# First layer of a recurrent-attention-plus-feed-forward kernel: the contraction of 384 split into seven products with 128-row and 64-row tiles

## The chip, the cores and the metric

The kernel runs on one core of one Trainium2 chip. The metric is the device time of one execution in microseconds (us). Everything is computed in float32. TensorE multiplies a stationary tile (`lhsT`, at most 128 rows by 128 columns) with a moving tile (`rhs`) and accumulates in PSUM; VectorE (DVE), ScalarE (ACT) and GpSimd (POOL) do the element work; SP and ACT issue the DMAs.

## The reference

Two blocks follow one another. The first is a recurrence over 768 tokens for 4 batches and 8 heads of size 48:

```
for t in range(S):
    cur = einsum('bhd,bhe->bhde', u * kt, vt)
    y[:, :, t] = einsum('bhd,bhde->bhe', rt, state + cur)
    state = wt[..., None] * state + einsum('bhd,bhe->bhde', kt, vt)
```

Its output, seen as `x` of 3072 tokens by 384, goes through a feed-forward block: `h = x @ w_in` (384 to 2048), `g = h * sigmoid(h)`, `out = g @ w_out` (2048 to 384).

## The kernel before

The work is cut into 12 units. A unit is 128 tokens of two batches, so 256 rows of `x`. A unit has an attention stage (the recurrence in a logarithmic form over levels 0 to 6, with masks), a first layer (`ups`) and a second layer (`downs`). The order of all instructions is written by hand: the loop over `i` from 3 to 11 takes the attention stage of unit `i` as a list of groups (`mix(i)`), and between the groups it puts steps of the second layer of unit `i - 2` and then the first layer of unit `i - 1`; `room` says how many steps follow each group. Every engine runs its own instructions in that order. After the loop come the second layer of unit 10, and the first and second layers of unit 11, with no attention beside them.

The second layer is a matrix product in seven quarter-size products instead of eight (`quarter`, numbered here q0 to q6; line 1156), for units 1 to 11. It needs sums of activations (`sums`, L1127) on DVE. The results of the products share PSUM banks: q0, q2, q4 and q6 accumulate into one bank, and between them ACT or DVE copies the partial sum out (L1161, L1164). So q4 can start only when ACT's copy after q2 is done.

The first layer of units 0 to 2 is plain (`up`, L1011). From unit 3 on (`NFAST = 3`) it is `first_layer` (L1065): `w_in` and `x` have three chunks of 128 rows. Chunks 0 and 1 form the two halves of a seven-product scheme over (half of the 2048 columns) x (chunk) x (batch). The third chunk is multiplied plainly, as four more products, named by where they are accumulated: in `p7`, `p3`, `p4` and `n1`. Every matmul there takes 128 rows, 64 columns of weights and 128 tokens; two neighbours fill the lower and the upper 64 columns of the array. A "block" below is 8 such matmuls of one half of the features; the trace shows each float32 matmul as two records, so a block is 16 records. There are 11 products of two blocks each, 22 blocks a unit.

`keep_banks` gives the first layer four PSUM banks (`h0`, `h1`, `o0`, `o1`). Partial results are copied by ACT (L1074), added by DVE (L1077) and put through Silu by ACT (L1080, L1082). The sums of `x` that the scheme needs are `sums_of_x` (L1039, DVE); those of the weights are `in_weight_sums` (L1032, DVE, once).

The attention stage meets TensorE at `burst(i, 3)` and `burst(i, 5)` (L692: 48-row by 64-column tiles, 64 moving columns, a row tile for each head parity), at `turn_apart` (L811), `y_state` (L835, L842), `y_values` (L856) and `update` (L896). Between burst 3 and burst 5 the keys of the next levels go from ACT (`odd_keys`, L604) to POOL (`grow_keys`, L634) and the queries through DVE (L616, L771) and ACT (L773). After burst 5, ACT copies scores out of PSUM (`keep_level`, L792), and `y_state` waits for that. `move_x` brings the attention's output into the layout of `x` by ten DMAs, from ACT's queue (L928), two in group 0 and eight in group 1. `load_blocks` (L127), `load_values` (L140, L147), `load_rk` (L157) and the outputs (L1170) are on SP's queue. `block_bonus` (L491, POOL) and `block_sum` (L525, DVE) make the terms inside blocks of eight tokens.

Of the kernel before, what the change touches and what calls it, by code (L numbers as in the profile page):

```python
# [38 lines left out]
def kernel(  # L39
# [56 lines left out]
    WRK = {"w": 0, "r": 1, "k": 2}  # L96
    vt, vq, whole = {}, {}, {}
# [32 lines left out]
    def load_values(i):  # L130
        n, b0 = units[i]
        t0 = n * L

        rooms = [pin.tile([128, H * D + PD - D], F32, name=name, bufs=2) for name in ("vt", "vq")]
        if n == 0:
            for room in rooms:
                nc.vector.memset(room[:, H * D:], 0.0)
        whole[i] = rooms
        vt[i], vq[i] = (room[:, 0:H * D].rearrange("p (h d) -> p h d", h=H) for room in rooms)
        nc.sync.dma_start(out=vt[i], in_=v[b0, :, t0:t0 + L, :].rearrange("h t d -> t h d"))  # L140
        if i < NTOK:
            nc.sync.dma_start(out=vq[i], in_=v[b0 + 1, :, t0:t0 + L, :].rearrange("h t d -> t h d"))
            return

        for g in range(4):
            t1 = t0 + L - (g + 1) * 32
            nc.sync.dma_start(out=vq[i][g * 32:(g + 1) * 32], in_=v[b0 + 1, :, t1:t1 + 32, :].rearrange("h t d -> t h d"))  # L147
# [666 lines left out]
    def turn_k(i):  # L814
        both_kq = pt.tile([128, NB, NP, 2 * PD], F32, name="kq", bufs=1)
        for b in range(NB):
            kq[i, b] = both_kq[:, b]
        for e, have in enumerate(apart[i]):
            nc.scalar.copy(out=both_kq[:, :, :, PD * e:PD * e + D], in_=have)
# [46 lines left out]
    def x_products(i, b):  # L866

        if b == 0:
            xt[i] = pt.tile([128, KC, TU], F32, name="xt", bufs=1)
# [18 lines left out]
    def update(i, b):  # L888
# [5 lines left out]
        for p in range(NP):  # L894
            for e in range(2):
                nc.tensor.matmul(p_kv[i][PD * e:PD * e + D, b, p, :], lhsT=kq[i, b][:, p, PD * e:PD * e + D],  # L896
# [17 lines left out]
    def move_x(i, first=0, last=None, queue=nc.sync):  # L914

        if i not in xt:
            xt[i] = pt.tile([128, KC, TU], F32, name="xt", bufs=1)
        moves = []
        for h in range(H):
            at = h * D  # L920
            while at < (h + 1) * D:
                end = min((h + 1) * D, (at // 128 + 1) * 128)
                row = PD * (h % 2) + at - h * D
                moves.append((xt[i][at % 128:at % 128 + end - at, at // 128, :],
                              yt[i][row:row + end - at, h // 2].rearrange("p b t -> p (b t)")))
                at = end
        for to, have in moves[first:last]:
            queue.dma_start(out=to, in_=have)  # L928

# [8 lines left out]
    def mix(i):  # L938
# [15 lines left out]
        def start(j):  # L954
# [4 lines left out]
                (sums, i - 1, FH // 2 - 2 if i - 1 < NFAST else 0), *both(update, i), *at(not ahead, (move_x, i))]]  # L959
# [24 lines left out]
        if i + 1 < len(units):  # L984
            loads.insert(len(loads) // 2, (load_values, i + 1))
# [36 lines left out]
    HALF = DF // 2  # L1022
    whole_w = raw[:, 1].rearrange("p x b h d -> p x (b h d)")
    in_sums = [whole_w[:, WRK["r"]], const.tile([128, HALF], F32, name="in_sum"), whole_w[:, WRK["w"]]]
    a11, a12, a13 = (w_in_sb[:, c, 0:HALF] for c in range(KC))
    a21, a22, a23 = (w_in_sb[:, c, HALF:DF] for c in range(KC))
    x_sums = [spare[:, at + x * L:at + (x + 1) * L] for x in range(3)] + [const.tile([128, L], F32, name="x_sum")]

    def in_weight_sums(which):
        out, one, two, op = ((in_sums[0], a21, a22, ALU.add), (in_sums[1], in_sums[0], a11, ALU.subtract),  # L1030
                             (in_sums[2], a12, in_sums[1], ALU.subtract), (a21, a11, a21, ALU.subtract))[which]
        nc.vector.tensor_tensor(out=out, in0=one, in1=two, op=op)  # L1032

    def sums_of_x(i):

        (b11, b12), (b21, b22), (b31, b32) = (tuple(xt[i][:, c, b * L:(b + 1) * L] for b in range(NB)) for c in range(KC))
        d1, d2, d4, d3 = x_sums
        for out, one, two in ((d1, b12, b11), (d2, b22, d1), (b12, b22, b12), (d4, b21, d2), (d3, b31, b32)):
# [10 lines left out]
    def first_layer(i, half, *names):  # L1049

        (b11, b12), (b21, b22), (b31, b32) = (tuple(xt[i][:, c, b * L:(b + 1) * L] for b in range(NB)) for c in range(KC))
        d1, d2, d4, d3 = x_sums
        s1, s2, s4 = in_sums
        for name in names:
            place, first, last, pairs = {
                "p1": ("x", True, True, [(a11, b11)]), "p6": ("x", False, True, [(s2, d2)]), "p7": ("x", False, True, [(a21, b12), (a23, b32)]),
                "p4": ("x", False, True, [(a22, d4), (a23, d3)]), "p5": ("y", True, True, [(s1, d1)]),
                "p3": ("y", False, True, [(s4, b22), (a13, b32)]), "p2": ("z", True, False, [(a12, b21)]),
                "n1": ("z", False, True, [(a13, b31)])}[name]
            p = kept[{"x": ("h0", "h1"), "y": ("o0", "h0"), "z": ("o1", "o1")}[place][half]][:].rearrange("p (q t) -> p q t", q=4)  # L1060
            for n, (left, right) in enumerate(pairs):
                for q in range(4):
                    for h in (0, PD):
                        f = (4 * half + q) * 128 + h
                        nc.tensor.matmul(p[h:h + PD, q, :], lhsT=left[:, f:f + PD], rhs=right, start=first and n == 0 and q == 0,  # L1065
                                         stop=last and n == len(pairs) - 1 and q == 3, skip_group_check=True)

            def g(x, b):
                if (i, x, b, half) not in gt:
                    gt[i, x, b, half] = pt.tile([128, 4, L], F32, name="gt", bufs=FC // 2)  # L1070
                return gt[i, x, b, half]

            if name in ("p1", "p6", "p5"):
                nc.scalar.copy(out=g(*{"p1": (0, 0), "p6": (0, 1), "p5": (1, 1)}[name]), in_=p)  # L1074
            elif name in ("n1", "p7", "p3"):
                to = g(*{"n1": (0, 0), "p3": (0, 1), "p7": (1, 1)}[name])
                nc.vector.tensor_tensor(out=to, in0=p, in1=to, op=ALU.add)  # L1077
                if name == "p3":
                    gt[i, 0, 1, half] = p
                nc.scalar.activation(out=gt[i, 0, 1, half] if name == "p3" else to, in_=to, func=AF.Silu)  # L1080
            elif name == "p4":
                nc.scalar.activation(out=g(1, 0), in_=p, func=AF.Silu)  # L1082

    def out_room(b):
# [3 lines left out]
        return temps.rearrange("p a b e -> p (a b e)").bitcast(F32)[:, 4 * FH * L:4 * FH * L + DM]  # L1088
# [18 lines left out]
    quarters = temps.rearrange("p a b e -> p (a b e)").bitcast(F32)[:, 0:4 * FH * L].rearrange("p (s f t) -> p s f t", s=4, f=FH)  # L1107
# [7 lines left out]
    def sums(i, m):  # L1115

        if i >= NFAST:
            lower, upper = ([gt[i, x, b, m] for b in range(NB)] for x in range(2))
            lower, upper = ([t[:, :, :] for t in have] for have in (lower, upper))
            s1, s2, s3, s4 = (quarters[:, x, 4 * m:4 * m + 4, :] for x in range(4))  # L1120
        else:
            lower, upper = (gt[i, x].rearrange("p a (b t) -> p b a t", b=NB) for x in (m, m + FH // 2))
            lower, upper = ([have[:, b] for b in range(NB)] for have in (lower, upper))
            s1, s2, s3, s4 = (quarters[:, x, 2 * m:2 * m + 2, :] for x in range(4))
# [191 lines left out]
```

## Time and profile before

| what | value |
|---|---|
| times of three executions | 588.58, 589.61, 592.87 us |
| median | 589.61 us |
| profiled execution, span from first to last instruction | 588.6 us (the profile lists no other time for it) |
| granted TensorE clock | 1.000 |
| busy TensorE matmul / weight load | 573.7 / 533.3 us |
| busy VectorE / GpSimd / ScalarE | 455.7 / 354.1 / 264.2 us |
| L1156, three groups of the page, busy | 88.8 + 59.9 us, and the smaller ones |
| L1065, two groups of the page, busy | 62.8 + 46.9 us, and the smaller ones |
| L1011, busy | 66.1 us |

The page gives busy times by engine and by line; a line's busy time on TensorE is the time during which at least one of its matmuls ran. Because matmuls overlap, the cost of a block is read best from the timeline, as the distance from its start to the start of the next block. "PEld" is the weight load; a wait shown there is a wait of TensorE's queue for an operand or a bank.

### The profile page before, as it was taken

How to read it: one execution, taken by the hardware profiler on the slowest of the kernel's cores; microseconds unless marked ns; L12 is line 12 of the kernel's file. 1: busy time of each engine (PE TensorE's matmuls, PEld its weight loads, DVE VectorE, ACT ScalarE, POOL GpSimd, SP SyncE). 2: the span in 40 equal slices, each digit the busy share in tenths (PEclk: the TensorE clock that was granted, in tenths of full speed). 3: DMA queues.
4: the chain of work that ended last, by engine and by line, in shares of the span. 5: the costliest groups of instructions: out<-in, count | busy, mean ns of one | idle time of the engine just before them, and what ended most of it. 6: DMA issues, size and time to landing. Idle time of an engine off the chain costs nothing.

```text
span 588.6 us, 19384 instructions
## 1 busy us (share of the span) xinstructions
PE 573.7 (97%) x8070; PEld 533.3 (91%) x8070; DVE 455.7 (77%) x703; ACT 264.2 (45%) x582; POOL 354.1 (60%) x415
## 2 busy tenths in 40 slices
PE   8989999999999999999999999999999989999997
PEld 8767876798899989999999989999999989999997
DVE  7979789998898898787788898888678797861150
ACT  5679694431531561561561561460470462370320
POOL 5989778357768478287486496485676677500000
PEclk9999999999999999999999999999999999999999
DMA  9957785343432643544543544444354460100000
GB/s 231 311 122 195 167 244 82 47 86 70 102 68 39 133 71 53 131 66 75 114 68 60 123 62 68 105 75 73 85 100 71 95 102 27 38 7 24 28 3 26
DMA packets 203383, 53.70 MB, mean 91 GB/s; under 512 B 186784, under 2 KB 195104, under 8 KB 203296
## 3 DMA queue, kind: packets, MB, share of 16 engines
q1 hardware_dynamic: 197360, 48.73, 41.0%
q10 hardware_dynamic: 5936, 3.74, 2.4%
q8 instruction: 63, 1.03, 0.8%
q14 instruction: 24, 0.20, 0.1%
HBM read 43.21 MB, written 5.24 MB: 82 GB/s over the span
## 4 chain that ended last, share of the span: by engine, by line
PE 76%; SPq 5%; DVE 5%; POOL 4%; DMA 4%; ACT 3%; issue 1%; ACTq 1%; POOLq 0%; DVEq 0%
PE p_o L1156 26%; PE p_h L1065 16%; PE p_o L1065 8%; PE p_h L1011 8%; PE p_h L1156 4%; PE p_m L1095 4%; PE p_m L856 2%; PE p_sc L692 2%; DVE score L561 2%; SPq L127 2%; PE p_m L835 2%; DMA vq<-in_v_dram 2%; ACT score L792 2%; POOL w_in_sb L259 2%; POOL tk L634 1%
## 5 line engine op out<-in xcount | busy, mean ns | idle before, releaser
L634 POOL TENSOR_TENSOR tk<-tk,tw 128x256 f32<-128x256 f32 x128 | 91.3, 734 | 42.8 <-ACT tk L604 27.6
L491 POOL TENSOR_TENSOR ruk<-tokens_rk 128x768 f32<-128x768 f32 (+1 forms) x32 | 53.6, 1687 | 70.9 <-DVE block_sums L525 36.6
L1156 PE MATMUL p_o<-own,temps 128*128 128x192 f32 x528 | 88.8, 327 | 1.3 <-ACT partial L1161 1.3
L1156 PEld LDWEIGHTS p_o<-own,temps 128*128 128x128 f32 x528 | 86.0, 190 | 2.5 <-ACT partial L1161 2.4
L1011 PE MATMUL p_h<-xt,w_in_sb 128*128 128x256 f32 x288 | 66.1, 384 | 1.7 <-POOL w_in_sb L259 1.5
L1065 PE MATMUL p_h<-xt,w_in_sb 128*64 128x128 f32 x1008 | 62.8, 274 | 0.4 <-issue 0.4
L1011 PEld LDWEIGHTS p_h<-xt,w_in_sb 128*128 128x128 f32 x288 | 53.6, 190 | 10.0 <-POOL w_in_sb L259 2.4
L1156 PE MATMUL p_o<-w_out_sb,gt 128*128 128x192 f32 x340 | 59.9, 329 | 0.2 <-DVE temps L1127 0.2
L616 DVE TENSOR_TENSOR tr<-tr,tw 128x512 f32<-128x512 f32 x61 | 57.3, 939 | 2.6 <-PE p_m L692 2.1
L1065 PEld LDWEIGHTS p_h<-xt,w_in_sb 128*64 128x64 f32 x1008 | 55.8, 137 | 2.0 <-issue 0.9
L1156 PEld LDWEIGHTS p_o<-w_out_sb,gt 128*128 128x128 f32 x340 | 55.3, 190 | 2.0 <-issue 1.2
L1161 ACT COPY partial<-p_o 128x192 f32<-128x192 f32 x33 | 10.6, 320 | 95.7 <-PE p_o L1156 46.5
L406 POOL TENSOR_TENSOR tw<-tw 128x256 f32<-128x256 f32 (+6 forms) x83 | 40.0, 482 | 17.7 <-DVE tw L360 13.8
L1065 PE MATMUL p_o<-xt,w_in_sb 128*64 128x128 f32 x720 | 46.9, 273 | 0.0
L604 ACT COPY tk<-tk 128x256 f32<-128x256 f32 x52 | 21.2, 407 | 53.8 <-POOL tk L634 49.2
L1065 PEld LDWEIGHTS p_o<-xt,w_in_sb 128*64 128x64 f32 x720 | 40.8, 137 | 0.0
L1074 ACT COPY gt<-p_h 128x512 f32<-128x512 f32 x45 | 26.2, 582 | 30.4 <-PE p_h L1065 30.4
L1080 ACT ACTIVATE gt<-gt 128x512 f32<-128x512 f32 x36 | 22.7, 631 | 34.1 <-DVE gt L1077 33.9
L710 DVE COPY_PREDICATED score<-mask,p_sc 128x512 f32<-128x512 int8 x42 | 31.3, 800 | 5.8 <-PE p_sc L692 5.5
L1077 DVE TENSOR_TENSOR gt<-p_o,gt 128x512 f32<-128x512 f32 x27 | 18.4, 683 | 19.4 <-PE p_o L1065 19.4
L1077 DVE TENSOR_TENSOR gt<-p_h,gt 128x512 f32<-128x512 f32 x27 | 18.6, 687 | 17.3 <-PE p_h L1065 16.2
L643 POOL TENSOR_TENSOR tk<-tk,tw 128x256 f32<-128x256 f32 x32 | 30.9, 986 | 0.0
(225 smaller groups left out, 1272.0 us busy)
## 6 DMA issues: line engine op xcount, KB each, us to landing
w_out_sb<-in_moe_w_in_dram SPq DMA_DIRECT2D x6, 768.0 KB, 7.1
w_out_sb<-in_moe_w_out_dram SPq DMA_DIRECT2D x4, 768.0 KB, 5.1
own<-in_moe_w_out_dram SPq DMA_DIRECT2D x4, 768.0 KB, 5.8
tokens_rk<-in_r_dram SPq DMA_DIRECT2D x8, 384.0 KB, 4.4
tokens_rk<-in_k_dram SPq DMA_DIRECT2D x8, 384.0 KB, 5.3
tokens_w<-in_w_dram SPq DMA_DIRECT2D x8, 384.0 KB, 6.4
raw<-in_w_dram SPq DMA_DIRECT2D x80, 32.0 KB, 2.3
raw<-in_k_dram SPq DMA_DIRECT2D x80, 32.0 KB, 2.1
```

Of the source, the lines that this page charges most:

```text
L406: engine.tensor_tensor(out=up, in0=t[:, :, 0::2], in1=t[:, :, 1::2], op=ALU.mult)
L491: mul = lambda out, one, two: nc.gpsimd.tensor_tensor(out=out, in0=one, in1=two, op=ALU.mult)
L616: nc.vector.tensor_tensor(out=odd, in0=odd, in1=tw[i][l][:, :, 0::2][:, :, :, None].to_broadcast([128, Q, L >> (l + 1), c]), op=ALU.mult)
L634: nc.gpsimd.tensor_tensor(out=out, in0=have, in1=odd_products(i, l, b, *blocks), op=ALU.mult)
L643: nc.gpsimd.tensor_tensor(out=have, in0=have, in1=odd_products(i, l, b, [2, NP * ni]), op=ALU.mult)
L710: nc.vector.copy_predicated(out=dst, mask=masks[l][:, :, None].to_broadcast([128, NB, NP, ni, c]), data=sc[e].rearrange("p (b q) (i c) -> ...
L1011: nc.tensor.matmul(p_h[:, a, :], lhsT=w_in_sb[:, c, f * 128:(f + 1) * 128], rhs=xt[i][:, c, :], start=(c == 0), stop=(c == KC - 1))
L1065: nc.tensor.matmul(p[h:h + PD, q, :], lhsT=left[:, f:f + PD], rhs=right, start=first and n == 0 and q == 0, stop=last and n == len(pairs) ...
L1074: nc.scalar.copy(out=g(*{"p1": (0, 0), "p6": (0, 1), "p5": (1, 1)}[name]), in_=p)
L1077: nc.vector.tensor_tensor(out=to, in0=p, in1=to, op=ALU.add)
L1095: nc.tensor.matmul(po[i, b], lhsT=gt[i, f // 2][:, f % 2, b * L:(b + 1) * L], rhs=w_out_sb[:, f, :], start=(f == 0), stop=(f == FC - 1))
L1156: nc.tensor.matmul(p, lhsT=left(f), rhs=right[:, f, :], start=which in (0, 1, 3) and f == 0, stop=f == FH - 1, skip_group_check=True)
```

## The change

The third chunk of 128 rows is split in two halves of 64 rows, and one half is put with chunk 0, the other with chunk 1. So the seven-product scheme covers all 384 rows (192 + 192), and the four plain products are gone. Each of the seven products has 16 matmuls with 128 rows as before ("whole rows") and 16 matmuls with 64 rows ("half rows"). For those, the features' first half takes rows 0 to 63 and its second half takes rows 64 to 127, and they alternate with the lower and upper 64 columns, so that four neighbours lie in four different quarters of the array; the two row halves write different PSUM banks. In `p2`, `p5` and `p3` half rows come first, in the others whole rows.

What this needs beside it: `x` gets a fourth room, in which chunk 2's halves lie in both row halves (`spread_x`, two ACT copies); `move_x` has eleven DMAs; blocks of `w_in`'s third chunk change places between the row halves once (`swap_out` on SP, `swap_in` on ACT); `sums_of_x` has four operations on 256 columns instead of five on 128 and moves from group 3 to group 4; of the four weight sums, now 1024 + 512 columns each, two go to POOL. Rooms are found by keeping three instead of four quarters of `sums` (the fourth goes over the result of `p3`), and one room for the values instead of two. From unit 5 on block loads are spread over the groups by a table; `load_values(i)` is issued in the stage that uses it. The first layer is seven steps, so `room` changes.

```diff
+    x_rooms = const.tile([128, KC + 1, TU], F32, name="x_rooms")
+    s1_room = const.tile([128, HALF + BW], F32, name="in_sum")
+    value_rooms = const.tile([128, NB, H * D], F32, name="values")
...
-        rooms = [pin.tile([128, H * D + PD - D], F32, name=name, bufs=2) for name in ("vt", "vq")]
+        have = s1_room if i == 1 else value_rooms.rearrange("p x d -> p (x d)")
+        rooms = [have[:, b * H * D:(b + 1) * H * D] for b in range(NB)]
...
+        ends = [128, 256, 384] if i < NFAST else [128, 256, 320, 384]
...
+    def spread_x(i):
+        lower, upper = slice(0, PD), slice(PD, 2 * PD)
+        nc.scalar.copy(out=x_rooms[upper, 2], in_=x_rooms[lower, 2])
+        nc.scalar.copy(out=x_rooms[lower, 3], in_=x_rooms[upper, 3])
...
+        if i > NPAIR:
+            for place, some in enumerate(("w", "ww", "wvr", "r", "", "rr", "k", "k", "k", "k")):
...
-        for out, one, two in ((d1, b12, b11), (d2, b22, d1), (b12, b22, b12), (d4, b21, d2), (d3, b31, b32)):
+        for out, one, two in ((d1, b12, b11), (d2, b22, d1), (b12, b22, b12), (d4, b21, d2)):
...
-    def first_layer(i, half, *names):
-                "p1": ("x", True, True, [(a11, b11)]), "p6": ("x", False, True, [(s2, d2)]), "p7": ("x", False, True, [(a21, b12), (a23, b32)]),
-                "p4": ("x", False, True, [(a22, d4), (a23, d3)]), "p5": ("y", True, True, [(s1, d1)]),
-                "p3": ("y", False, True, [(s4, b22), (a13, b32)]), "p2": ("z", True, False, [(a12, b21)]),
-                "n1": ("z", False, True, [(a13, b31)])}[name]
+    def first_layer(i, name):
+            "p1": ("h", True, a11, b11, False), "p2": ("o", True, a12, b21, True), "p6": ("h", False, s2, d2, False),
+            "p5": ("o", True, s1, d1, True), "p7": ("h", False, a21, b12, False), "p3": ("o", False, s4, b22, True),
+            "p4": ("h", False, a22, d4, False)}[name]
+        whole_rows = [(half, q, h, slice(0, 128), left[0][:, half * BW + q * 128 + h:half * BW + q * 128 + h + PD], right[:, 0])
+                      for half in range(2) for q in range(4) for h in (0, PD)]
+        half_rows = [(half, q, h, rows, left[1][rows, q * 128 + h:q * 128 + h + PD], right[rows, 1])
+                     for q in range(4) for h in (0, PD) for half, rows in enumerate((slice(0, PD), slice(PD, 128)))]
+        for n, part in enumerate((half_rows, whole_rows) if turned else (whole_rows, half_rows)):
...
-            order = (((0, "p1"), (0, "p5"), (0, "p2")), ((0, "p6"), (0, "n1"), (1, "p1")), ((0, "p7"), (0, "p3")),
-                     ((0, "p4"), (1, "p2"), (1, "p6")), ((1, "p5"), (1, "n1")), ((1, "p7"),), ((1, "p3"),), ((1, "p4"),))
+            made = [[(first_layer, i, name)] for name in ("p1", "p2", "p6", "p5", "p7", "p3", "p4")]
...
-            groups[3].append((sums_of_x, i - 1))
+            groups[3].append((spread_x, i - 1))
+            groups[4].append((sums_of_x, i - 1))
...
+        if i == NFAST + 1:
+            groups[0].append((swap_in, 0))
+            groups[2].insert(0, (in_weight_sums, 3))
+            groups[3].insert(0, (in_weight_sums, 1))
+            groups[5].append((in_weight_sums, 2))
-        room = (1, 1, 0, 2, 1, 1, 1, 1, 1, 2, 2, 1, 1) if i < NPAIR else (2, 1, 2, 2, 1, 1, 1, 2, 1, 1, 1)
+        room = (1, 1, 0, 2, 1, 1, 1, 1, 1, 2, 2, 1, 1) if i < NPAIR else (2, 1, 2, 2, 1, 1, 1, 1, 1, 1, 1)
```

## The prediction

> **What bounds the kernel now.** I read the page first. Its engine line and the first row of its slices say that TensorE is busy from end to end at full clock; its chain that ended last is three quarters TensorE.
>
> ```profile
> PE 573.7 (97%) x8070; PEld 533.3 (91%) x8070; DVE 455.7 (77%) x703; ACT 264.2 (45%) x582; POOL 354.1 (60%) x415
> ...
> PE   8989999999999999999999999999999989999997
> ```
>
> So the change is worth what it does to TensorE's own time plus what it adds or takes away in waits. For the first I went to the timeline of TensorE around a burst of unit 7 (start, duration, then the group with its count of records):
>
> ```profile
> 337.32 1.04 PE L1065 MATMUL p_h<-spare,raw 128*64 128x128 f32 x16
> 338.19 1.04 PE L1065 MATMUL p_o<-xt,w_in_sb 128*64 128x128 f32 x16
> 339.16 0.69 PE L692 MATMUL p_sc<-tr,tk 48*64 48x64 f32 x32
> 339.68 0.65 PE L692 MATMUL p_m<-tr,tk 48*64 48x64 f32 x32
> 340.25 1.97 PE L1065 MATMUL p_h<-xt,w_in_sb 128*64 128x128 f32 x32
> 342.05 1.04 PE L1065 MATMUL p_h<-xt,raw 128*64 128x128 f32 x16
> ```
>
> Starts are what counts, since durations overlap. A block of 16 records costs 338.19 - 337.32 = 0.87 us. Going over to the 48-row tiles makes the block before it 339.16 - 338.19 = 0.97. The 32 records of L692 have 64 moving columns instead of 128; the first 32 take 0.52, the next 0.57, and the two L1065 blocks behind them 1.80 instead of 1.74.
>
> The second view is the waits, longest first. TensorE's, after the first units, are few:
>
> ```profile
> PEld p_m L835 <- ACT score L792: 3.8, 7, 1.4
> ...
> PEld p_o L1156 <- ACT partial L1161: 2.4, 4, 1.1
> ```
>
> The rest of a unit's 45 us is the second layer (seven products of 2.6 us, 18.2), the first layer (22 x 0.872 = 19.2) and some 7 us of attention. The kernel is at TensorE's floor for this list of matmuls; DVE and POOL have idle time, but their chains decide whether TensorE finds its operands.
>
> **The products.** Removed: 22 blocks a unit, 22 x 0.872 = 19.18 us. Added: seven products with two whole-row blocks each, 14 x 0.872 = 12.21, and seven sets of 16 half-row matmuls (32 records). Do four half-row matmuls run at a time? The nearest row is `y_state`: 48-row, 48-column tiles with the same 128 moving columns, spread over the four quarters, 32 records:
>
> ```profile
> 390.11 1.13 PE L835 MATMUL p_m<-tr,state 48*48 48x128 f32 x32
> 391.02 0.22 PE L842 MATMUL p_m<-score,vt 64*48 64x64 f32 x1
> ```
>
> From its start to the next line's, 0.91 us for 32 records, where L1065 needs two blocks, 1.74, for as many. L692, with half the columns, needs 0.52 for its first 32. Both are four at a time. L692 even has the new loop's order of neighbours and its two banks. So a half-row set costs one block's 0.87: 7 x 0.872 = 6.10. Total 18.31, which is 0.87 us a unit less, 7.9 us over nine units.
>
> But each of the seven products now changes once between tiles of 128 rows and of 64. From the first timeline: into the small tiles the block before grows by 0.10 (0.97 against 0.87), and the first 32 records take 0.05 more than a set in mid-stream would (0.52, where 8 groups at the pace of L1065's 0.109 us a pair, halved for 64 columns, make 0.44 to 0.47). Back again, the last 32 take 0.10 more and the next two blocks 0.06 more. So 0.15 us for a change in either direction. `p2`, `p5` and `p3` are turned round, so that between products no further change arises, and what stands at the bursts, at `turn_apart` and ahead of q0 was a change before too. 7 x 0.15 = 1.05 us a unit. The products then cost 19.36 a unit against 19.18: +0.18, times nine **+1.6 us**. Bounds: 0.10 a change (the shift of the start alone) gives -1.6; 0.20 gives +4.8. I take 0.15, since the row has both parts.
>
> The Trainium skill speaks against the change at just this place: "TensorEngine Tiling (Array Packing)", section Key Properties, says that changing the tiling mode, not merely the tile, drains TensorE. It has no price; the row's 0.15 us agrees with it. By the page's 2x for a contraction of 64 and no drain the sum would be -7.9 us, by row and rule together +1.6.
>
> **Waits of `y_state`.** They come because ACT copies the scores of burst 5 (L792) late, behind a Silu that waits for DVE. Between burst 5 and `turn_apart` TensorE had four blocks (3.5 us); it gets `p7` and `p3`, 2 x (2.61 + 0.15) = 5.5 us. ACT's queue ahead of the copies is now the copies of `p5` (2 x 0.59), no Silu. The copies take 2.1 + 1.5 us plus a little; starting 0.2 to 1.4 us after burst 5 they are done by about 5 us. **-3.8 us**; bounds -3.8 to 0.
>
> **ACT's queue and q4.** Eight DMAs of `move_x` stand in front of the copy after q2, and q4 waits for it:
>
> ```profile
> 308.66 6.88 ACTq L928 DMA_DIRECT2D xt<-yt  x8
> 315.58 0.32 ACT L1161 COPY partial<-p_o 128x192 f32<-128x192 f32 x1 [7.57 <-DMA xt<-yt]
> 315.95 2.57 PEld L1156 LDWEIGHTS p_o<-own,temps 128*128 128x128 f32 x16 [0.80 <-ACT partial L1161]
> ```
>
> There are nine now. In other units the eight take 5.0 to 6.1 us, so a DMA is 0.63 to 0.86. In half of the units there is more than a microsecond to spare, in the other half none: up to 4 x 0.75 = +3.0 us. Against it: SP's 16 key loads, issued in these very microseconds before (11 of them in 7.28 us from 307.76), are now issued in groups 6 to 9, some 20 us earlier; in their place come the 16 loads of `w`, which can start as soon as DVE has transposed the last `w`, near 301. And `p4` is 0.9 us longer between the transposition and q0. I take **0**, bounds -2.4 and +5.1 (0.64 x 8).
>
> **`spread_x` and `sums_of_x`.** Two ACT copies of 64 x 256, about 0.4 us each by L604's 0.41 for 128 x 256, in a stretch where ACT is idle 4 us (it waits for POOL before L604); hidden. `sums_of_x` took DVE 320.29 to 326.0 in unit 7, drawn out by POOL's 1.87 us operations. It now stands behind the block sums: by the same rows the second block sum ends 3.7 us after burst 3, four operations end near 5.5, masks and L616 near 7.4, the additions for `p2` near 8.8. `p6` needs `d2` at 6.5 and `p5` its banks at 9.3. Hidden, with half a microsecond left at `p5`; if DVE is later than that, `p5` waits for the excess.
>
> **The weight sums in unit 4.** Two of 1024 + 512 columns go to POOL; 768 columns take it 1.87 us, so one is about 3.7. The first stands ahead of the level 2 and 3 keys:
>
> ```profile
> 178.76 2.41 POOL L491 TENSOR_TENSOR ruk<-tokens_rk 128x384 f32<-128x384 f32 x2 [3.62 <-DVE block_sums L525]
> ...
> 183.45 3.11 POOL L634 TENSOR_TENSOR tk<-tk,tw 128x256 f32<-128x256 f32 x4
> ...
> 188.72 0.65 PE L692 MATMUL p_m<-tr,tk 48*64 48x64 f32 x32
> ```
>
> The keys are done at 186.56 and would be at 190.2, 1.5 us late for level 4 of the burst; DVE, rid of its own 1.21 us weight sum at 176.0, releases POOL 1.2 us sooner. About 0.3 there, and perhaps 0.7 for `p5` behind later block sums. The second stands in POOL's 4 us of idle time ahead of L634 in group 6. **+1.0**, bounds 0 and +5.
>
> **The rest.** In the last unit the scores of `p3` now lie in the banks that q0 takes, so q0 waits for two `sums`: +0.3. Values have one room: `load_values` waits for `update` of the unit before, and has from there to group 6 before `reverse_v` needs it; hidden by more than 20 us. The DVE weight sums that leave unit 3, the memsets and the swaps of `w_in` (0.64 each on ACT's queue, ahead of a copy that waits 2 us for q0 anyhow) lie beside TensorE: 0.
>
> Sum: 1.6 - 3.8 + 0 + 1.0 + 0.3 = -0.9 us against the span of 588.6. The median of the runs is 1.0 above that span, so 589.6 - 0.9 = 588.7.
>
> **The rivals.** *Faster: waits go and drains are cheap.* A change costs 0.10 (-1.6), the waits of `y_state` and q4 vanish (-6.2), and the order of loads also takes away the 3 us or so of small waits that the trace shows at the bursts: 589.6 - 11 = 579. For it: those waits come from late loads and late ACT copies. Against it: 0.05 more is plain in the row, both ways. 0.22.
>
> *Slower: burst 5 waits.* Burst 3 to burst 5 was 339.16 - 323.95 = 15.2 us; now it is 1.1 for the burst and four products, 4 x 2.76, so 12.2. The keys for it come last:
>
> ```profile
> 332.72 0.41 ACT L604 COPY tk<-tk 128x256 f32<-128x256 f32 x1
> 333.27 1.19 POOL L634 TENSOR_TENSOR tk<-tk,tw 128x256 f32<-128x256 f32 x2 [4.00 <-ACT tk L604]
> ```
>
> They were done at 334.46, 10.5 us after burst 3: 4.7 us to spare, now 1.7. L604 stands behind ACT's Silus of `p2`, and those behind DVE's additions; in my working they end 0.5 us later than now. If that chain slips by more than 1.7 us, TensorE pays the excess in units 4 to 11. A slip of 4 makes 8 x 2.3 = +18: 608; of 3, +10: 600. 0.15.
>
> *Slower: the half rows don't run four at a time* but two: 7 x 9 x 0.872 = +55, 644. L692 and L835 speak against it. 0.03.
>
> **How the numbers follow.** Forecast 0.60, the faster case 0.22, the slower ones 0.18. About 1% (5.9 us) is what a measurement can tell from no change; the forecast's own range, 584 to 595, lies inside it. So faster 0.22, same 0.60, slower 0.18. The range reaches into both neighbours, 580 to 599: at the low end nearly all of the first rival, at the high end a slip of 3 us at burst 5; about 0.1 is left out on either side.
>
> **What would show it.** In the profile after: half-row sets of 32 records at 0.87 to 0.92 us, each product 2.7 to 2.8 from start to start (2.6 would be the faster case, 3.5 the last one); no wait at `y_state` for L792; burst 5 without a wait for L634, 12 us after burst 3; q4's wait unchanged; a wait of about 1 us in unit 4 for POOL. A wait of over a microsecond in every unit, or a product above 2.9 us, would make the prediction wrong.

## The result, and the profile after

The changed kernel took 628.0 us (median of four runs, 627.5 to 629.6) beside 591.2 us for the kernel before in the same comparison (588.6 to 595.8): a ratio of 1.062, with a 95% interval of 1.057 to 1.068. The forecast was 588.7 us and a range of 580 to 599. The profiled execution of the changed kernel has a span of 625.8 us, 37.2 more than before. In the medians of all experiments, executions more than 1.5% above the fastest of the same kernel are left out.

The page first (busy times, then the slices of TensorE and its granted clock):

```profile
PE 587.0 (94%) x8934; PEld 532.7 (85%) x8934; DVE 441.3 (71%) x690; ACT 268.5 (43%) x600; POOL 361.5 (58%) x419
...
PE   8989999999797899997998997999898999999998
...
PEclk9989999999998899999998999899999999999999
```

TensorE is busy 13.3 us longer than before, but its share falls from 97% to 94%: its slices go down to 7 tenths, where before had 8 or 9 up to the last one, and the clock is down to 8 tenths in some (before it was granted in full). So most of the loss is waits and a slower clock, not a longer list of products.

The products themselves went as the prediction had them. TensorE around burst 5 of unit 6 (start, duration, group):

```profile
305.41 1.92 PE L1100 MATMUL p_h<-spare,raw 128*64 128x128 f32 x32
307.26 1.10 PE L1100 MATMUL p_h<-spare,temps 64*64 64x128 f32 x32
308.19 2.95 PE L1100 MATMUL p_o<-spare,in_sum 64*64 64x128 f32 x64
311.07 0.69 PE L695 MATMUL p_sc<-tr,tk 48*64 48x64 f32 x32
```

`p6` is 32 whole-row records (two blocks) and 32 half-row records, 308.19 - 305.41 = 2.78 us, and the half rows take 0.93 from start to start: four at a time. In the last unit, where its products wait for nothing, the first layer takes 604.19 - 584.61 = 19.58 us from its start to the start of q0, against 567.04 - 547.37 = 19.67 before. But the 19.67 hold a wait of q0 for VectorE, which the row after doesn't have:

```profile
567.04 2.87 PE L1156 MATMUL p_o<-w_out_sb,gt 128*128 128x192 f32 x16 [0.24 <-DVE temps L1127]
```

So it is 19.58 against 19.43, 0.15 us more; the prediction had 0.18.

Where the time went shows in the list of waits (waiter, what it waited for: total us, times, longest):

```profile
ACT partial L1206 <- DMA x_rooms<-yt: 56.5, 9, 8.1
...
PEld p_o L1201 <- ACT partial L1206: 22.4, 12, 3.2
...
PE p_o L1201 <- ACT partial L1206: 18.7, 11, 2.9
...
PE p_h L1031 <- ACT gt L1040: 3.5, 1, 3.5
```

The wait that was to go, `y_state` for the scores of burst 5, has gone (its weight loads still wait 0.3 us for ScalarE). In its place the second layer (L1201) waits for ScalarE's copies between its products, and ScalarE for the moves of `x`. By units, from the start of `y_state` to the next one's start (worked out from the starts of L835 in the trace before and L838 after):

| unit | 3 | 4 | 5 | 6 to 10, sum | 11 |
|---|---|---|---|---|---|
| before | 45.7 | 45.6 | 45.0 | 226.2 | 43.6 |
| after | 49.6 | 53.7 | 47.6 | 248.5 | 43.1 |
| difference | +3.9 | +8.1 | +2.6 | +22.3 | -0.5 |

The sum is +36.4 of the 37.2. Three places are to be explained: unit 3, unit 4, and the steady units from 5 on.

The steady units first. Stage 7 of the trace after, where the second layer of unit 5 follows the first layer of unit 6, from three answers of the timeline (SP's queue, ScalarE with its queue, TensorE):

```profile
304.04 1.00 SPq L550 DMA_DIRECT2D spare<-kept  x2
305.17 1.52 SPq L160 DMA_DIRECT2D tokens_rk<-in_r_dram  x1
...
308.02 5.84 SPq L132 DMA_DIRECT2D raw<-in_r_dram  x8
313.90 10.45 SPq L132 DMA_DIRECT2D raw<-in_k_dram  x16
324.45 9.24 SPq L132 DMA_DIRECT2D raw<-in_w_dram  x16
```

```profile
330.72 1.62 ACTq L931 DMA_DIRECT2D x_rooms<-yt  x2
332.43 0.32 ACT L1206 COPY partial<-p_o 128x192 f32<-128x192 f32 x1 [5.79 <-DMA raw<-in_w_dram]
333.23 6.87 ACTq L931 DMA_DIRECT2D x_rooms<-yt  x9
340.14 0.32 ACT L1206 COPY partial<-p_o 128x192 f32<-128x192 f32 x1 [7.39 <-DMA values<-in_v_dram]
```

```profile
325.44 2.87 PE L1201 MATMUL p_o<-w_out_sb,gt 128*128 128x192 f32 x16
...
332.80 7.15 PE L1201 MATMUL p_o<-own,temps 128*128 128x192 f32 x32 [1.90 <-ACT partial L1206]
```

The same place in the kernel before:

```profile
303.27 4.44 SPq L127 DMA_DIRECT2D raw<-in_r_dram  x8
304.78 2.87 PE L1156 MATMUL p_o<-w_out_sb,gt 128*128 128x192 f32 x16
305.24 1.69 ACTq L928 DMA_DIRECT2D xt<-yt  x2
```

In the kernel after, q0 starts at 325.44, and the first two moves of `x` could start half a microsecond later, as they did before (305.24 - 304.78). They start at 330.72. The copy of q0's result stands behind them on ScalarE and comes at 332.43, so q2 waits 2 us; the other nine moves are done at 340.1, so q4 waits too. And q2 with q3, 5.36 us at full clock, take 7.15: for 3.4 of them (a window, in what follows) TensorE has half its clock. The table by windows shows that (time, then busy time of each engine, then PEclk):

```profile
333.20:336.60 3.40, 3.40 (x13) 3.40 (x12) 3.03 (x4) 0.00 (x0) 1.92 (x2) 0.51 0.73 137
```

The bracket behind the copy at 332.43 names a `w` load on SP's queue. Why a move of `x` should wait for a `w` load, which has nothing to do with its data, is in the compiled program's list of waits. Every DMA there waits, beside its operands, for one of eight semaphores, and the DMAs of both queues take these in turn, in the order that the scheduler assumed. So each DMA waits until the DMA eight places ahead of it (its holder, below) has landed, whichever queue that is on. The trace shows it: eight semaphores tell of the landings of all these DMAs; the seventh `w` load, issued at 328.77, landed at 330.64, and the first move was issued at 330.72; the ninth landed at 331.75, and the second move came at 331.82. For the moves of `x` of a steady unit (which load holds the semaphore, counted within its kind; "own": another move):

| kernel | first two moves | third, fourth | the rest | loads from `load_rk` to the first holder |
|---|---|---|---|---|
| before | `r` loads 1 and 3 of the second eight | `r` load 7, own | `k` loads 1, 2, 4, 5, 6 and own | 8 w + 8 r + 5 v + 1 = 22 |
| after | `w` loads 7 and 9 | `w` loads 12 and 13 | `w` load 15, values 1 and 2, own | 8 r + 16 k + 7 w = 31 |

SP issues its DMAs one after another, 40 loads in 333.7 - 308.0 = 25.7 us here, 0.64 each, and the row begins behind `load_rk`. That stands on SP's queue behind the three DMAs of the block sums (`spare<-kept` above are the last two), which wait for VectorE and for each other, and is issued at 305.17, some 20 us ahead of q0 (before: 18.5 us). The 22nd load is out in time, the 31st is not. That is theory A. The rival B: eleven moves instead of ten and two spreading copies make ScalarE's queue too long by themselves, or the transfers get in each other's way.

### The profile page after: what moved, and what is told of

Read it like the earlier page. It is cut to its first block, busy times and chain, and to the rows that moved or that the text cites. A ratio compares the mean times of both kernels' runs of the same rounds, so it can differ in the third digit from the quotient of the medians.

```text
span 625.8 us, 21222 instructions
## 1 busy us (share of the span) xinstructions
PE 587.0 (94%) x8934; PEld 532.7 (85%) x8934; DVE 441.3 (71%) x690; ACT 268.5 (43%) x600; POOL 361.5 (58%) x419
## 5 line engine op out<-in xcount | busy, mean ns | idle before, releaser
L1031 PE MATMUL p_h<-x_rooms,w_in_sb 128*128 128x256 f32 x288 | 68.0, 392 | 4.2 <-ACT gt L1040 3.5
L1201 PE MATMUL p_o<-own,temps 128*128 128x192 f32 x352 | 63.0, 340 | 9.6 <-ACT partial L1206 9.6
L1201 PEld LDWEIGHTS p_o<-own,temps 128*128 128x128 f32 x352 | 60.5, 199 | 11.3 <-ACT partial L1206 11.3
L1031 PEld LDWEIGHTS p_h<-x_rooms,w_in_sb 128*128 128x128 f32 x288 | 54.7, 194 | 13.2 <-ACT gt L1040 3.9
L619 DVE TENSOR_TENSOR tr<-tr,tw 128x512 f32<-128x512 f32 x61 | 64.7, 1060 | 0.5
L1201 PE MATMUL p_o<-w_out_sb,gt 128*128 128x192 f32 x340 | 59.9, 329 | 0.0
L1100 PE MATMUL p_h<-x_rooms,w_in_sb 64*64 64x128 f32 (+1 forms) x1152 | 56.0, 278 | 1.4 <-issue 1.3
L1201 PEld LDWEIGHTS p_o<-w_out_sb,gt 128*128 128x128 f32 x340 | 55.3, 190 | 1.7 <-issue 1.2
L1100 PEld LDWEIGHTS p_h<-x_rooms,w_in_sb 64*64 64x64 f32 (+1 forms) x1152 | 48.0, 136 | 6.4 <-issue 5.3
L1201 PE MATMUL p_o<-own,gt 128*128 128x192 f32 x172 | 32.2, 343 | 9.3 <-ACT partial L1206 9.2
L1201 PEld LDWEIGHTS p_o<-own,gt 128*128 128x128 f32 x172 | 29.5, 199 | 11.1 <-ACT partial L1206 11.0
L1112 ACT COPY gt<-p_h 128x512 f32<-128x512 f32 x36 | 19.2, 585 | 34.6 <-PE p_h L1100 34.6
```

The lines of the kernel that those rows point to most:

```text
L619: nc.vector.tensor_tensor(out=odd, in0=odd, in1=tw[i][l][:, :, 0::2][:, :, :, None].to_broadcast([128, Q, L >> (l + 1), c]), op=ALU.mult)
L1031: nc.tensor.matmul(p_h[:, a, :], lhsT=w_in_sb[:, c, f * 128:(f + 1) * 128], rhs=xt[i][:, c, :], start=(c == 0), stop=(c == KC - 1))
L1100: nc.tensor.matmul(banks_of[half][h:h + PD, q, :], lhsT=weights, rhs=have, start=first and n == 0 and q == 0, stop=n == 1 and q == 3, skip ...
L1201: nc.tensor.matmul(p, lhsT=left(f), rhs=right[:, f, :], start=which in (0, 1, 3) and f == 0, stop=f == FH - 1, skip_group_check=True)
```

## The experiments

All times are device microseconds; the kernel before was run beside each.

**Old order of loads in the new kernel.** `a_oldloads`:

```diff
-        if i > NPAIR:
+        if False:
             count = {"w": 0, "r": 0, "k": 0}
```

> The kernel after, with the table of block loads switched off: from unit 5 on the loads are spread over groups 2 to 10 as in the kernel before, and load_values(i) stands in group 1. Nothing else differs. Theory A (the table puts the w loads on SP's queue just ahead of the moves of x; SP issues one DMA in about 0.6 us and is behind, and each move waits for the DMA eight places ahead of it, a w or values load): the waits of L1201 for ACT L1206 fall from 41 us to under 15, the halved clock behind them goes, and the time is 600 to 612 us. Theory B (the ninth to eleventh DMA of x, spread_x and the longer ACT queue make q2 and q4 late, whatever the loads do): 620 to 630 us, with q2 and q4 waiting as now.

Measured: 635.3 us (634.1 to 637.5; 1.074 of before, interval 1.069 to 1.079). Theory A as it was written there fell: the old order is worse, 257.2 us for units 6 to 10. But the moves' waits show what they stand behind:

```profile
323.94 9.00 SPq L132 DMA_DIRECT2D raw<-in_k_dram  x16
```

```profile
331.72 1.21 ACTq L931 DMA_DIRECT2D x_rooms<-yt  x2
333.03 0.32 ACT L1206 COPY partial<-p_o 128x192 f32<-128x192 f32 x1 [6.53 <-DMA raw<-in_k_dram]
```

Now it is the `k` loads. In the wait list the first two moves here hang on `k` loads 11 and 12, which are the 35th and 36th load behind `load_rk`. The values, which before stood in the middle of the row, now come behind the `k` loads (41st to 45th), and the moves come later in the row than before; why the scheduler puts them there is not shown. Not "`w` ahead of the moves" is the cause, but how late on SP's queue the holder is: theory A2.

**New order of loads in the old kernel.** `b_newloads` puts the new table into the kernel before, nothing else (`load_values(i + 1)` where the table has "v").

```diff
+        if i > NPAIR:
+            for place, some in enumerate(("w", "ww", "wvr", "r", "", "rr", "k", "k", "k", "k")):
...
+                        groups[place].append((load_values, i + 1))
```

> The kernel before with the new table of block loads alone, from unit 5 on; the values of the next unit are loaded where the table has the values, into the two rooms that they have there. First layer, moves of x and all else as before. Theory A: q2 and q4 (L1156) wait for ACT L1161 in every unit from 6 on, 2 to 4 us a unit, some of it doubled by a halved clock: 605 to 620 us. Theory B: the table costs nothing by itself, 588 to 595 us.

Measured: 601.6 us (601.4 to 602.3; ratio 1.017, 1.012 to 1.022), 9.5 us over before, short of A's 605 and far from B's 588 to 595. The first layer, the ten moves and ScalarE's copies are those of before, and yet the weight loads of L1169 (the second layer there) wait 8.6 us for the copies, in five waits, against 2.4 in four before; units 6 to 10 take 232.1 us. (Another 5.1 us are in unit 5, where `p6` waits 3.3 us for a Silu on ScalarE; the copies ahead of it there wait 3.2 us for a DMA of the block sums on SP's queue.) The table alone costs something, since the first holders are `w` loads 2 and 4, the 26th and 28th load: later than 22, earlier than 31. (In unit 6 the holders are still the 20th and 22nd, and that unit loses nothing, 44.8 us.)

**All but `k` ahead of `load_rk`.** `a_vfirst` decides it:

```diff
-            for place, some in enumerate(("w", "ww", "wvr", "r", "", "rr", "k", "k", "k", "k")):
+            for place, some in enumerate(("v", "ww", "wwr", "rrr", "", "k", "k", "k", "k", "")):
```

> The kernel after with another order in the table of block loads, nothing else: values first (group 0), then the 16 w and the 16 r loads in groups 1 to 3, ahead of load_rk, and only the 16 k loads behind load_rk (groups 5 to 8). In the old order, as in after, 40 loads stand behind load_rk, 0.6 us each on SP's queue, which brings them 27 us later, into the moves of x; here 16 stand there, and end about 10 us after load_rk, before q0. In the program's wait list each move of x now waits for the DMA eight places ahead, which is a k load for the first two, a load of values or one of the first five w loads for the others. Theory A2 (what counts is how late on SP's queue the DMA eight places ahead of each move is): the waits of L1201 for ACT L1206 fall from 41 us to under 12, and the time to 600 to 612 us. Rival B (eleven moves on ACT's queue are themselves too slow, or the transfers of the loads hold them up): waits as in after, 620 to 632 us.

Measured: 605.5 us (603.7 to 609.2; ratio 1.023, 1.016 to 1.030). Units 6 to 10 take 226.3 us, as before the change (226.2). The same stage as above:

```profile
308.18 12.25 SPq L132 DMA_DIRECT2D raw<-in_k_dram  x16
...
325.14 12.03 SPq L132 DMA_DIRECT2D raw<-in_w_dram  x16
```

```profile
325.82 0.56 ACTq L931 DMA_DIRECT2D x_rooms<-yt  x1
...
328.51 0.32 ACT L1206 COPY partial<-p_o 128x192 f32<-128x192 f32 x1 [1.70 <-PE p_o L1201]
...
334.47 0.32 ACT L1206 COPY partial<-p_o 128x192 f32<-128x192 f32 x1 [5.64 <-DMA raw<-in_w_dram]
```

Here too 16 `w` loads are issued from 325 on, at the same time as the moves and as in after. But the holders of the first two moves are `k` loads 14 and 15, out by 320.4, and the moves start 0.2 us after q0 (325.60). All eleven moves and both spreading copies are in this kernel, and so is the traffic: rival B, both halves of it, is out. The eight shared semaphores and the place of the holder on SP's queue are what cost the 22 us, the half clock that followed the waits included. (Over four orders the first holder's place, 14, 26, 31 and 35, goes with 226, 232, 249 and 257 us for units 6 to 10; before has 22 and 226. Units 3 to 5 of `a_vfirst` are slow, 51.4, 50.7 and 49.2 us; the table does not reach them.)

**Unit 4: who pays for the weight sums.** `a_sums_dve` puts the two sums of GpSimd on VectorE (`nc.gpsimd` becomes `nc.vector` twice).

```diff
-                                     (s4, a12, s2, ALU.subtract, nc.gpsimd), (a21, a11, a21, ALU.subtract, nc.gpsimd))[which]
+                                     (s4, a12, s2, ALU.subtract, nc.vector), (a21, a11, a21, ALU.subtract, nc.vector))[which]
```

> The kernel after with the two weight sums of GpSimd back on VectorE (same places in the order). If the two POOL sums of unit 4 cost what the trace after shows around them (waits of 3.4 and 0.8 us at burst 3, 1.6 us at p5, and two windows of 3.4 us at half clock, up to 1.7 us each): 619 to 624 us. Rival: VectorE, which has 1024 + 512 columns twice more to add in the same stretch, becomes as late as GpSimd was: 626 to 630 us, with waits on L1117 or L619 in unit 4 instead.

Measured: 627.2 us (625.0 to 630.5), not to be told from after. Yet unit 4 falls from 53.7 to 48.0. In after, GpSimd works on the first sum until 194.2 and TensorE stands at burst 3:

```profile
189.76 4.46 POOL L1065 TENSOR_TENSOR w_in_sb<-w_in_sb 128x1024 f32<-128x1024 f32 x2
...
195.52 0.69 PE L695 MATMUL p_sc<-tr,tk 48*64 48x64 f32 x32 [3.18 <-POOL tk L637]
```

On VectorE the burst has no wait. `p5` then waits 2.05 us where it waited 1.43, behind additions that are now behind a weight sum. So the time is the rival's, and its mechanism is there in part. What unit 4 gave, unit 5 took (50.9 instead of 47.6, with a wait of 2.2 us at q2): its moves stand behind the loads that unit 4 issues in the old order (first holder the 36th load).

**Price of a change between tiles.** `a_alternate` cuts each product in four pieces instead of two:

```diff
-        for n, part in enumerate((half_rows, whole_rows) if turned else (whole_rows, half_rows)):
+        order = (half_rows, whole_rows) if turned else (whole_rows, half_rows)
+        for n, part in ((n, [x for x in order[n] if x[1] // 2 == some]) for some in range(2) for n in range(2)):
```

> The kernel after, with each product's matmuls in four pieces instead of two: 8 whole rows, 16 half rows, 8 whole rows, 16 half rows (or the other way round), so three changes between tiles of 128 and 64 rows in a product instead of one, 14 more in a unit. If a change costs the 0.15 us that the prediction took: the first layer of the last unit, which waits for nothing, goes from 19.58 to 21.7 us, and the whole by up to 9 x 2.1 = 19 us to about 645, less where units wait anyhow. If a change costs nothing, 19.6 and 628; at 0.10 each 21.0, at 0.20 each 22.4.

Measured, one run: 634.9 us. The first layer of the last unit takes 611.51 - 589.74 = 21.77 us instead of 19.58: 2.19 for 14 changes, 0.156 each. In the other units much of it fell into waits that were there anyhow, so the whole grew by 7, not 19.

**Waits of the steady units filled.** `a_filler` puts ten products of the identity ahead of q2 and of q4:

```diff
+        if i >= NFAST and which in (2, 4) and i < len(units) - 1:
+            beat(10)
```

> The kernel after with ten 128-column products of the identity on TensorE ahead of q2 and of q4 in units 3 to 10 (about 1.45 us by their row, 0.73 us for five), so that TensorE works for that part of its wait there; the loads and ACT's queue are as in after. If the windows of 3.4 us at half clock come from waits of some 2 us and cost up to 1.7 us each: the clock in these units stays full and the time falls by 4 to 8 us, to 620 to 624, although more matmuls run. If the windows come from anything else, or cost nothing: 628 to 632 us, windows as in after.

Measured: 631.3 us (628.7 to 633.0). In the profiled execution the windows at half clock are gone from the steady units (three there in after, none here). The other profiles say the same of units 6 to 10: four windows or more in `a_oldloads`, `a_sums_dve` and `a_values3`, which have the waits at q2 and q4, and none in `a_vfirst`, `a_best` and `a_final_noflip`, which don't. So they do come from TensorE's waits. But there was no gain. From `y_state` of unit 2 to that of unit 11, where 14 of the 16 fillers lie, ten products at 1.09 us add 15.3; TensorE's waits ahead of the second layer's products fall by 12.5 (18.8 to 6.3); three windows at up to 1.7 us are 5.1; and the waits at the bursts grow by 3.1 (4.9 to 8.0), some of them with no releaser in the profile. That makes +0.8, where the stretch took 443.0 us against 442.5. (The rest of the difference of the profiles lies in the first 120 us, which this does not touch, and behind the stretch, where the last two fillers are.) The price of a window fits 1.7 us; the 7.15 us above show it more plainly.

**Unit 3.** `a_vfirst_plus` has the sums on VectorE and `swap_in` a step later, on top of `a_vfirst`.

```diff
-            steps[11].insert(0, (swap_in, 1))
+            steps[12].insert(0, (swap_in, 1))
```

> As a_vfirst, and also all weight sums on VectorE and the first swap_in one step later on ACT's queue (step 12 of unit 3 instead of 11). If the waits of unit 4 at burst 3 (4.1 us in after, gone in a_sums_dve) and the wait of 3.65 us at L1031 in unit 3 (ACT behind a swap that waits for the tokens' loads) are each lost time of their own: 5 to 8 us less than a_vfirst, 594 to 606 us. If later waits take up what these give, within 2 us of a_vfirst.

Measured: 603.9 us (600.4 to 605.0), beside 605.5 for `a_vfirst`: mostly the second expectation. Unit 3 hardly moved (50.5 us, 51.4 in `a_vfirst`), and TensorE's wait at L1031 is still 2.8 us: the swap, which I had blamed for it, was not the main cause. The timeline of VectorE in after showed another:

```profile
146.52 0.01 DVE L404 LOAD_MASK_SELECT values<-values  x1 [5.21 <-DMA values<-in_v_dram]
```

`reverse_v` waits 5.2 us for the values of unit 3, and with it all of VectorE's queue, the block scores (L593, at 157.63 us), ScalarE's copies of them (which wait 3.9 us), and the Silu that frees TensorE's bank. Before, these values were loaded from 126.15 us on, ahead of the moves of `x`; with one room they are loaded from 141.28, behind ten moves and twelve `k` loads. `a_values3` loads them right behind the moves:

```diff
-        groups[0 if i < NPAIR else 1].append((load_values, i))
+        if i >= NPAIR:
+            groups[1].append((load_values, i))
...
-       (move_x, 2),
+       (move_x, 2), (load_values, 3),
```

> The kernel after, with the values of unit 3 alone loaded earlier: issued on SP's queue right behind the moves of x of unit 2, ahead of the last three block loads there, where after has them behind those loads. In the trace after, VectorE stands 5.2 us at reverse_v (L404) of unit 3 until these values land (146.5 us), everything VectorE does for burst 3 and the blocks comes as much later, ScalarE's copies L795 wait 3.9 us for it, and TensorE 3.65 us at L1031. Theory C (the late values are the whole loss of unit 3, 49.6 us from y_state to y_state against 45.7 in before): the wait at L1031 goes, unit 3 takes 45.5 to 46.5 us, and the whole 624 us. Rival (the swap of w_in on ScalarE's queue, which waits for the tokens' loads just ahead of the late Silu, holds the bank): unit 3 stays at 48.5 to 49.6 us.

Measured, one run: 623.7 us, and unit 3 takes 45.9; the wait at L1031 for the Silu is gone. Theory C holds.

```profile
141.11 0.01 DVE L404 LOAD_MASK_SELECT values<-values  x1
```

**All of it mended.** `a_best` takes the table of `a_vfirst` from unit 4 on, early values, and the sums on VectorE, two of them in groups 6 and 7.

```diff
-        if i > NPAIR:
+        if i >= NPAIR:
+            if i == NPAIR:
+                groups[0] += late
...
-            groups[2].insert(0, (in_weight_sums, 3))
...
-            groups[5].append((in_weight_sums, 2))
+            groups[6].append((in_weight_sums, 3))
+            groups[7].append((in_weight_sums, 2))
```

> The kernel after with four mendings of loads and weight sums, the products as in after: the table of loads of a_vfirst, used from unit 4 on; unit 3's values early as in a_values3; all weight sums on VectorE, the last two of them in groups 6 and 7 of unit 4. If the three places are all of the loss (table 25 us, unit 3 some 4.5, unit 4 and the first moves after it some 8): units of 45 to 46 us throughout and 588 to 594 us, level with before. If a fourth cause is left (spread_x, the extra moves, the products): 596 to 603 us.

Measured: 599.4 us (593.6 to 602.3; ratio 1.012, 1.008 to 1.016); the profiled execution has a span of 594.5. All units are at 43 to 46 us but unit 4, 51.4: the last sum came after the block scores, at 206.8 to 210.3, and `p3` waited 5.2 us for it. My place for it was bad.

`a_best_flip` turns the order of half and whole rows round in all seven products (`turned` True for `p1`, `p6`, `p7`, `p4`, False for the others).

```diff
-            "p1": ("h", True, a11, b11, False), "p2": ("o", True, a12, b21, True), "p6": ("h", False, s2, d2, False),
+            "p1": ("h", True, a11, b11, True), "p2": ("o", True, a12, b21, False), "p6": ("h", False, s2, d2, True),
...
```

> As a_best, with the order of half rows and whole rows turned round in all seven products, so that half rows stand beside the bursts, y_state and turn_apart, whose 48-row tiles are of the same kind. Counted from burst 3 to q0, the changes between 128-row and small tiles fall from 13 to about 7 a unit. At 0.15 us a change (0.156 in a_alternate): 0.9 us a unit, 7 to 8 us less than a_best, 580 to 587 us, faster than before. If 48-row tiles and 64-row tiles are not of one kind, or waits take the gain up: within 2 us of a_best.

Measured: 594.8 us (590.7 to 599.0; ratio 1.003, 0.999 to 1.007), 4.7 less than `a_best` where the count had 7 to 8. The profile does not show the gain: units 6 to 10 take 225.0 us, 224.8 in `a_best`, and unit 4 takes 55.6, since `p3` waits 9.7 us for the same late sum. The pair below does not bear the gain out either.

`a_final_noflip` has both sums in group 6 and the two late `k` blocks behind `load_rk`:

```diff
-                groups[0] += late
+                groups[5] += late
...
-            groups[6].append((in_weight_sums, 3))
-            groups[7].append((in_weight_sums, 2))
+            groups[6] += [(in_weight_sums, 3), (in_weight_sums, 2)]
```

> As a_best, with the last two weight sums of unit 4 both in group 6, where VectorE was idle for 3.5 us in a_best (in a_best the last one came at 206.8 to 210.3 us, and TensorE waited 5.4 us for it ahead of p3), and with the two late k blocks of unit 5 loaded behind load_rk instead of in front of everything. If that wait was all that was left in unit 4: 45.5 to 46.5 us for it instead of 51.4, and the whole 5 to 7 us less than a_best, 588 to 592 us in the profile, level with before. If the sums only move the wait to burst 5 or p7: within 2 us of a_best.

Measured: 590.2 us (588.2 to 593.1) beside 591.5 before: ratio 0.998, 0.995 to 1.001. The units are 45.9, 45.1, 46.3, then 224.7 for 6 to 10, and 43.1. The page has TensorE where it was before:

```profile
PE 573.7 (97%) x8934; PEld 524.1 (89%) x8934; DVE 427.7 (72%) x694; ACT 269.6 (46%) x600; POOL 349.9 (59%) x415
```

So the mendings of loads and weight sums take back all of the loss, and what is left of the change is level with the kernel before. From `y_state` of unit 2 to that of unit 11 it takes 405.0 us, 406.1 before. By TensorE's records there, start to start with idle time counted apart: the waits ahead of `y_state` are gone (2.35 us before), but those ahead of first-layer products are 2.35 us instead of 0.42, and the first layer itself takes 157.4 us instead of 155.7. The gain and the price of the changed scheme nearly cancel.

`a_final` is the same with the flags of `a_best_flip`.

> As a_final_noflip, with half rows and whole rows in the turned order of a_best_flip. In a_best_flip the stretch from burst 3 to burst 5 took less than in a_best, but units 6 and 7 lost 2.0 and 1.3 us at p7 in waits that nothing in the profile explains. If the turn is worth 0.5 to 0.9 us a unit: 4 to 7 us less than a_final_noflip, 582 to 587 us, faster than before by 0.5 to 1%. If such waits take it up: equal to a_final_noflip within 2 us.

Measured: 591.3 us (587.1 to 595.7; ratio 1.000, 0.997 to 1.004). From burst 3 to burst 5 of unit 9 it takes 427.40 - 415.32 = 12.08 us against 430.07 - 417.72 = 12.35: two changes less, 0.27 us, about as counted. But at `p7` TensorE waits up to 2.2 us in single units, in waits with no releaser in the profile (in unit 9, at 431.36, a window at half clock follows, and the unit takes 48.3 us instead of 44.6). What causes those stays open. No version beats the kernel before by more than the measurement can tell.

## Why the prediction was wrong

- *Products, +1.6 us*: right, and within its bounds. Half rows run four at a time (0.93), a change costs 0.156 where 0.15 was taken; the last unit's first layer grew by 0.15 us, and in `a_final_noflip`, without half clock, it grew by 1.7 between the `y_state` of unit 2 and of unit 11 (157.4 against 155.7), where the sum has 0.18 for each of eight units. The rival with two at a time is out.
- *`y_state`, -3.8*: right; the wait for the scores is gone. The 3.8 are waits of the weight loads; TensorE's own idle time there was 2.35 us.
- *`spread_x` and `sums_of_x`, 0*: right; `p5` waits for VectorE in unit 4 alone.
- *Burst 5 late* (the rival at 600 to 608): did not happen. TensorE has no wait there in the steady units.
- *ACT's queue and q4, taken as 0, bounds -2.4 to +5.1*: this is the step that failed, by some 25 us with unit 5 (+22.3 and +2.6). The prediction argued that the `w` loads "can start as soon as DVE has transposed the last `w`, near 301". That is when their room is free, not when SP comes to them: SP issues in order, 24 loads stood between `load_rk` and the first `w`, and they started at 324.45. The key loads did move ahead of q0, as it said (by 14.5 us, not 20: they start 11.5 us ahead of q0 instead of 3.0 behind it); but the loads that took their place became the ones that the moves wait for. And the bounds were counted from ScalarE's own DMAs (eight at 0.64); a move waiting for a DMA of another queue was not among the mechanisms considered, though the trace before had its sign: copies behind `xt<-yt` waiting up to 7.6 us with the SP queue busy.
- *Weight sums in unit 4, +1.0, bounds 0 to +5*: too small. The sum was put at 3.7 us and took 4.46; it began only at 189.76, when the prediction had the keys nearly done (190.2), and the keys came behind it. Unit 4 lost 8.1, of which the sums' place on GpSimd is 5.7 (53.7 to 48.0, though unit 5 then took most of it back).
- *One room for the values, 0, "hidden by more than 20 us"*: wrong in unit 3, +3.9. The values wait not only for `update` but for all that SP has ahead of them.
- *q0 in the last unit, +0.3*: not there. The trace after has no wait at that q0; before had 0.24 us.
- *The clock*: nowhere in the sum. Six windows of 3.4 us at half clock follow waits in the trace after; the profiled execution of the kernel before has none.

With loads and weight sums in their new places, `a_final_noflip` comes to 0.998 of before (0.995 to 1.001). The forecast of -0.9 us is 0.998 too; that interval does not tell it from no change, but the loss is gone with the same products, so it came from the order of the loads and the place of the weight sums.

The Trainium skill ("DMA: Bandwidth & Descriptors", section "Anatomy of one DMA — SWDGE (gpsimd) path") says that a DMA engine never waits for a semaphore; the sequencer that issues the DMA does, before it sends it. The section is on DMAs that GpSimd issues; the moves here are ScalarE's, and the trace agrees for them: the move waits on ScalarE's queue, and ScalarE stands idle for 5.79 us ahead of the copy behind it.

## What to carry to other kernels

When loads are reordered, follow the queue, not only the buffers: write down what stands ahead of each load on its own queue, at the measured time of one issue, from the last thing that holds that queue. Then look in the program's waits for DMAs of other queues that share a semaphore with it, since a transfer can be held by one that it has nothing to do with. And a room that is taken away moves a load to a later place: look for that place in the first units too, not only in the steady ones.

## What the runs showed of the hardware

Waits of TensorE shorter than a window can cost more than their length. After waits of 1.4 to 3.2 us (the shortest 1.43, at 208.94) the granted clock was 0.5 for 3.413 us, six times in the trace after. Other waits as long (1.84 at 282.64, 2.61 at 290.72, 3.49 at 164.41) were followed by none. Chance has a part in it: every profile of this case has the same wait of 1.5 to 1.7 us near 40 us from the start, and a window follows it in 8 of the 14, not in the other 6, the kernel before among them. The Trainium skill ("TensorE: Matmul & The Clock Gate") gives a window of 3413 ns that runs free of the kernel (section "What's actually happening"), and the rule that no idle gap should be longer than about 3.4 us (section "HAM oscillation — how this bites in real kernels"). The window agrees with the records here (the six start whole multiples of 3.413 us apart); the limit does not, since gaps of less than half that length were enough.

A change between tiles of 128 and of 64 rows costs 0.156 us (`a_alternate`).
